# Routed attention and a cosine router on one Trainium2 core: weight sums in four 32-row strips, spread by GpSimd, and routing work in other turns

## The chip, the core and the metric

The kernel runs on one core of a Trainium2 chip. Its engines are TensorE (PE in the profile, with PEld for its weight loads), VectorE (DVE), ScalarE (ACT), GpSimd (POOL) and SyncE (SP, which here only issues DMAs). The metric is device time in microseconds (us), the median of the runs shown. Lower is better.

## What is computed

The input is four batches of eight heads, 768 tokens of width 64. Each query and each key is given to the nearest of 16 centroids of its head; a query attends only to keys of its own centroid. The result, as 3072 rows of width 512, goes to a router that picks one of eight experts by cosine similarity, and each row passes through the two layers of its expert.

```
mask   = q_assign[:, :, :, None] == k_assign[:, :, None, :]
scores = where(mask, scale * q @ k^T, -1e9)
attn   = exp(scores - max);  attn = attn / (sum(attn, axis=-1) + 1e-9)
x      = (attn @ v) as (B*S, H*D)
logits = x_n @ emb_n^T / tau;  e = argmax(logits);  gate = softmax(logits)[e]
out    = gate * (relu(x @ w1[e]) @ w2[e])
```

The part that the change touches is the denominator, the sum of the attention weights of each query, and the order in which the router's small operations are put between the attention's.

## The kernel before

**Tiling.** Two heads are taken together, which gives 16 pairs, numbered here 0 to 15; four pairs make a batch, and `n`, `nb` and `b` in the code are the pair, the pair within its batch and the batch. A pair's queries are cut into two halves of 384 columns. For each half there are six units, one for each block of 128 keys. Six units that belong to one half of one pair are a group; there are 32 groups, 0 to 31, and group 2n + half belongs to pair n. The main loop takes two units at a time. This text calls that a turn: a pair has turns 0 to 5 (`it` in the code), turns 0 to 2 for its first group and 3 to 5 for its second.

**A turn.** In a turn the code issues, in this order: the scores of the next two units (L355, key cluster match in bf16 and then the product in f32, both heads side by side) and their exponentials on ACT (L366); what `between` puts there; in some turns `divide`; then for the turn's own two units `attend` (L375, weights times v into `o_ps`, and DVE adds the weights into `acc`, L384 and L394); in turns 0 and 3 at the end, `total` of the group that has just ended. The order on PE, DVE and ACT is the order in which the code issues the work (a manual schedule); each engine works its queue in order. POOL's order is set by the scheduler.

**The denominator.** `total` (L397) multiplies `acc` by a matrix of ones with two matmuls, one for each head, whose 64 output rows all hold the same sums (L402). ACT copies the 128x384 result out of PSUM (L410) and DVE takes its reciprocal (L411) into `den`. `divide` (L419) multiplies `o_ps` by `den` into `xT`; `rows` (L436, L441) transposes `xT` into the rows `xr`. `o_ps` and the PSUM bank `misc` have two buffers each, `prob` has five, `acc` and `den` two. In the last pair, group 30's `divide` stands in turn 4 and its `rows` in turn 5; group 31's `total`, `divide` and `rows` come after the loop, between the first matmuls of the experts' layer (`hidden`, L739).

**What `between` places.** For the next pair: transposes of q and k (turns 5 and 0), sums of v on POOL and centroid products (turn 1), `assign` (turn 2: DVE L275 and L276, then a POOL product L277), `choose` (turn 3: DVE L283 and L284), one-hot transposes (turn 4). For the pair before: `rows` of its first group in turn 1, of its second in turn 2. For the batch before: `route_pieces`, that is `products` (L458), `norms` (ACT, L483), `logits` (L471, DVE L474), `choose` (five DVE operations L494 to L498, six POOL additions into `cumx` L500, a square root on ACT), `gate_scale` (four DVE operations L505 to L508), `gate_exp` and `gate_sum` (three DVE operations L515 to L517, and SP's DMA of the rows to `x_rows`, L518). In the last batch, pairs 14 and 15 also hold the first part of the sorting of tokens to experts (`early`): `ranks` (PE L548 and L555 read `cumx` and `eq`; DVE L563) in turn 3 of pair 14, `firsts` and `experts` (L573 to L606) in its turn 4, `dest` (L616 to L640) in its turn 5, `hot_blocks` and `hot_rows` (L650 to L658) in turns 0 to 2 of pair 15, and in its turn 3 `tokens` (L667, L676 to L680) and three indirect loads on POOL's queue (L695).

**After the loop** come 28 blocks of 128 tokens through `hidden` (L739, L746) and `result` (L755, L765, L766), with weights loaded by SP.

Of the kernel before, what the change touches and what calls it, by code (L numbers as in the profile page):

```python
# [9 lines left out]
F32 = mybir.dt.float32  # L10
# [8 lines left out]
P = 128  # L19
# [18 lines left out]
def kernel(  # L38
# [12 lines left out]
    nc = tc.nc  # L51

    B, H, S, D = q.shape
# [4 lines left out]
    NJ = S // P  # L58
    NHP = H // 2
    HS = S // 2  # L60
# [18 lines left out]
    const = ctx.enter_context(tc.tile_pool(name="const", bufs=1))  # L79
# [8 lines left out]
    embT = const.tile([P, KD, 2 * C], F32, name="embT")  # L88
    prefc = const.tile([P, C], BF16, name="prefc")
    prefe = const.tile([P, E], BF16, name="prefe")  # L90
    ones = const.tile([P, D], F32, name="ones")
    epsc = const.tile([P, 1], F32, name="epsc")
    io_i = const.tile([P, P], I32, name="io_i")
    io_b = const.tile([P, P], BF16, name="io_b")
# [20 lines left out]
    smp = ctx.enter_context(tc.tile_pool(name="smp", bufs=2))  # L115
# [14 lines left out]
    def misc():  # L130
        return psM.tile([P, 512], F32, tag="misc", name="misc")
# [4 lines left out]
    def load(n, names):  # L136
        b, hp = pairs[n]
        t = ld.setdefault(n, {})
        for nm in names:
            t[nm] = ldp.tile([P, NJ, 2, D], F32, tag=nm + "32", name=nm + "32")  # L140
            for h in range(2):
                nc.sync.dma_start(
                    out=t[nm][:, :, h],
                    in_={"q": q, "k": k, "v": v}[nm][b, 2 * hp + h].rearrange(
                        "(p j) d -> p j d", j=NJ
                    ),
                )
# [60 lines left out]
    bk = misc()  # L208
# [12 lines left out]
    bk = misc()  # L221
# [118 lines left out]
    GU = NJ  # L340
    units = [(n, hq, j) for n in range(len(pairs)) for hq in range(2) for j in range(NJ)]
    ngroups = len(units) // GU
# [54 lines left out]
    def total(g):  # L397

        d = gr[g]
        bk = misc()  # L400
        for h in range(2):
            nc.tensor.matmul(  # L402
                bk[D * h : D * h + D, 0:HS],
                lhsT=ones,
                rhs=d["acc"][:, h],
                start=True,
                stop=True,
            )
        d["den"] = smp.tile([P, HS], F32, tag="den", name="den")
        nc.scalar.copy(d["den"], bk[:, 0:HS])  # L410
        nc.vector.reciprocal(d["den"], d["den"])  # L411

    def divide(g):
        n, hq, _ = units[GU * g]
# [14 lines left out]
    def rows(g):  # L429

        n, hq, _ = units[GU * g]
        b, hp = pairs[n]
        U = NJ // 2
        bk = misc()
        for u in range(U):
            nc.tensor.transpose(  # L436
                bk[:, P * u : P * u + P], xT[b, hq][:, hp, P * u : P * u + P], ident
            )
        if b not in xr:
            xr[b] = xp.tile([P, NJ, XW], F32, tag="xr", name="xr")  # L440
        nc.scalar.copy(  # L441
            xr[b][:, U * hq : U * hq + U, P * hp : P * hp + P],
            bk[:, 0:HS].rearrange("p (u w) -> p u w", w=P),
        )
# [260 lines left out]
    def weights(j):  # L705
        part, c = (0, j) if j < KA else (1, j - KA)
        sp = (EngineType.SP,)
        e = nc.values_load(eblks[part][0:1, c : c + 1], engines=sp, min_val=0, max_val=E - 1)
        c = nc.values_load(echgs[part][0:1, c : c + 1], engines=sp, min_val=0, max_val=1)
        nc.sync.dma_start(  # L710
            out=w1s[j % 2],
            in_=moe_w1[ds(e, 1)].rearrange("o (c p) f -> p (o c) f", p=P),
            cond=c > 0,
        )
        nc.sync.dma_start(
            out=w2s[j % 2],
            in_=moe_w2[ds(e, 1)].rearrange("o (c p) d -> p (o c) d", p=P),
            cond=c > 0,
        )
# [60 lines left out]
    prepare, route = {}, {}  # L780
# [11 lines left out]
    def piece(n, name):  # L792
        if n < NP:
            if n not in prepare:
                prepare[n] = prep_pieces(n)
            prepare[n][name]()

    def between(n, it):
        b, nb = divmod(n, NHP)
        if it == 5:  # L800
            piece(n + 2, "turn0")
            if n + 1 == NP:
                route[b] = route_pieces(b)
                rows(2 * n)
                route[b][0](0)
        elif it == 0:
            piece(n + 1, "turn1" if n else "turn0")
        elif it == 1:
            piece(n + 1, "values")
            piece(n + 1, "products")  # L810
            if n > 0:
                rows(2 * n - 2)
        elif it == 2:
            piece(n + 1, "assign")
            if n > 0:
                rows(2 * n - 1)
        elif it == 3:
            piece(n + 1, "choose")
        elif it == 4:
            piece(n + 1, "hots")  # L820
        if b > 0:
            if nb == 0 and it == 3:
                route[b - 1] = route_pieces(b - 1)
                for half in range(2):
                    route[b - 1][0](half)
            j = NJ * nb + it - 3
            if 0 <= j < NJ:
                route[b - 1][2](j)
            if nb == 1 and it == 3:
                for half in range(2):  # L830
                    route[b - 1][1](half)
            if nb in (1, 2) and 0 <= j - NJ < 4:
                route[b - 1][3][j - NJ]()
        if b == B - 1 and (nb, it) in early:
            early[nb, it]()
        if b == B - 1 and (nb, it) == (3, 0):
            weights(0)
            weights(1)

    with tc.manual_schedule(engines={EngineType.PE, EngineType.DVE, EngineType.Activation}):  # L840
        for name in ("turn0", "turn1", "values", "products", "assign", "choose", "hots"):
            piece(0, name)
        load(1, "qk")
        for m in range(2):
            scores(m)
            expo(m)
        for i in range(0, len(units), 2):
            n, it = divmod(i // 2, NJ)
            if it == 0 and n + 1 < NP:
                load(n + 1, "v")  # L850
            if it == 4 and n + 2 < NP:
                load(n + 2, "qk")
            if it == 0 and n == 1:

                for w in range(2):
                    nc.sync.dma_start(
                        out=w1s[w], in_=moe_w1[0].rearrange("(c p) f -> p c f", p=P)
                    )
                    nc.sync.dma_start(
                        out=w2s[w], in_=moe_w2[0].rearrange("(c p) d -> p c d", p=P)  # L860
                    )
            for m in range(i + 2, min(i + 4, len(units))):
                scores(m)
                expo(m)
            between(n, it)
            if i % GU == 2 and i > GU:
                divide(i // GU - 1)
            if i + 2 == len(units):
                ats.close()
                tile_waits = {"side": "right", "reuse_waits": "tile"}  # L870
                psX = ctx.enter_context(tc.tile_pool(name="psX", bufs=1, space=PSUM, **tile_waits))
                turn_x(0, nc.scalar.copy, xp.tile([P, DM], F32, tag="acc", name="xTm"))
            for m in range(i, i + 2):
                attend(m)
            if i % GU == 0 and i > 0:
                total(i // GU - 1)
            if i == 0:
                piece(1, "turn1")
        at.close()
        mop = ctx.enter_context(tc.tile_pool(name="mop", bufs=2, **tile_waits))  # L880
        rtb = ctx.enter_context(tc.tile_pool(name="rtb", bufs=1, **tile_waits))
        psH = ctx.enter_context(tc.tile_pool(name="psH", bufs=3, space=PSUM, **tile_waits))

        products, logits, norms, (choose, *gates) = route[B - 1]
        pb = Places(1, rtb)
        hidden(0, (0,))
        total(ngroups - 1)
        divide(ngroups - 1)
        for j in range(NJ // 2):
            norms(j)  # L890
        hidden(0, (1,))
        turn_x(1, nc.scalar.copy)
        logits(0)
        rows(ngroups - 1)
        products(1)
        hidden(1, (0,))
        for j in range(NJ // 2, NJ):
            norms(j)
        logits(1)
        choose()  # L900
        hidden(1, (1,))
        for gate in gates:
            gate()
        fetch(3)
        turn_x(2, nc.scalar.copy)
        result(0, (0,))
        pb.ranks()
        pb.firsts()
        result(0, (1,))
        weights(2)  # L910
        pb.dest()
        pb.experts()
        hidden(2)
        pb.hot_blocks()
        pb.hot_rows(0, 1)
        result(1, (0,))
        turn_x(3, nc.scalar.copy)
        result(1, (1,))
        weights(3)
        hidden(3, (0,))  # L920
        pb.tokens()
        hidden(3, (1,))
# [72 lines left out]
```

## Time and profile before

| what | us |
|---|---|
| median of 3 runs | 855.54 |
| the runs | 854.64, 855.54, 858.0 |
| the profiled execution, its own time | 857.06 |
| its span in the profile | 855.3 |
| attention loop, from the first scores to the last group | about 20 to 434 |
| the experts' layer | about 430 to 855 |

| engine | busy us | share of the span |
|---|---|---|
| PE | 828.1 | 97% |
| PEld | 491.2 | 57% |
| DVE | 362.5 | 42% |
| ACT | 305.5 | 36% |
| POOL | 126.5 | 15% |

All times of the profile are of that one execution, in us from the start of its span unless marked ns. A matmul of f32 operands shows as two records, since PE makes two passes; the counts of the PE groups are of passes. A group of the profile is one line, engine and shape; its mean is that of one record. In a timeline the bracket behind a row is the time that the engine sat idle before it and what ended that. The granted clock of PE (PEclk) is a share of its full speed.

### The profile page before, as it was taken

What the parts mean: (1) busy time and instruction counts of PE and PEld (TensorE: products, weight loads), DVE (VectorE), ACT (ScalarE), POOL (GpSimd) and SP (SyncE); (2) the same over time, 40 slices, a digit from 0 to 9 for tenths busy, and PEclk for the clock granted to TensorE, in tenths of its full rate; (3) what the DMA queues carried; (4) which work ended last, traced back from release to release, by engine and by line L of the source; (5) the groups of instructions that cost most, each with busy time, mean ns of one, the idle gap of its engine ahead of it and who ended that gap; (6) DMA issues with size and microseconds to landing.
All of it is one profiled execution on the core that took longest, in us unless ns stands there. A gap on an engine that the chain in (4) does not pass through costs nothing.

```text
span 855.3 us, 12807 instructions
## 1 busy us (share of the span) xinstructions
PE 828.1 (97%) x5227; PEld 491.2 (57%) x5227; DVE 362.5 (42%) x521; ACT 305.5 (36%) x489; POOL 126.5 (15%) x172
## 2 busy tenths in 40 slices
PE   4999999999999999999899999999999999999995
PEld 2444444444444444444386767767676767767672
DVE  3577878787868877789835000000000000000000
ACT  3555556755567555665452111111111111111110
POOL 4010111211112111020101101011110101010100
PEclk9999999999999999999999999999999999999998
DMA  9922211242211422011127847748383747216410
GB/s 238 342 56 57 56 31 25 57 130 57 56 34 23 130 56 57 20 47 47 33 105 295 291 177 260 290 144 319 125 321 141 289 173 273 95 47 250 184 38 22
DMA packets 108781, 115.24 MB, mean 135 GB/s; under 512 B 77221, under 2 KB 77221, under 8 KB 108208
## 3 DMA queue, kind: packets, MB, share of 16 engines
q1 hardware_dynamic: 104064, 100.68, 37.0%
q0 software_dynamic: 4480, 13.65, 4.2%
q8 instruction: 43, 0.70, 0.3%
q14 instruction: 18, 0.15, 0.1%
q10 hardware_dynamic: 176, 0.05, 0.0%
HBM read 152.11 MB, written 13.64 MB: 194 GB/s over the span
## 4 chain that ended last, share of the span: by engine, by line
PE 49%; issue 25%; DMA 22%; DVE 2%; SPq 0%; POOL 0%; ACT 0%; POOLq 0%
PE s_ps L355 19%; DMA out_dram<-y,sidx 17%; PE o_ps L375 16%; PE misc L239 3%; DMA out_dram<-y,gidx 3%; PE misc L402 2%; PE h_ps L739 2%; DMA w1s<-in_moe_w_dram 2%; PE misc L436 2%; PE misc L297 1%; PE misc L254 1%; PE misc L267 1%; PE y_ps L755 1%; PE misc L458 1%; DVE den L411 1%
## 5 line engine op out<-in xcount | busy, mean ns | idle before, releaser
L739 PEld LDWEIGHTS h_ps<-xTm,w1s 128*128 128x128 f32 x1792 | 202.5, 192 | 24.2 <-DVE xTm L727 20.5
L739 PE MATMUL h_ps<-xTm,w1s 128*128 128x128 f32 x1792 | 207.9, 277 | 2.8 <-DMA w1s<-in_moe_w_dram 2.8
L755 PE MATMUL y_ps<-w2s,hT 128*128 128x512 f32 x448 | 201.1, 592 | 0.0
L366 ACT ACTIVATE prob<-s_ps 128x768 f32<-128x768 f32 x192 | 153.9, 810 | 125.2 <-PE s_ps L355 97.6
L727 DVE COPY xTm<-x_ps 128x512 f32<-128x512 f32 x24 | 16.6, 691 | 333.4 <-PE x_ps L725 333.4
L355 PE MATMUL s_ps<-qT,kT 64*128 64x384 f32 x768 | 157.7, 489 | 0.0
L375 PE MATMUL o_ps<-prob,v 128*64 128x384 f32 x768 | 145.1, 499 | 0.0
L394 DVE TENSOR_TENSOR acc<-acc,prob 128x768 f32<-128x768 f32 x128 | 129.8, 1014 | 3.6
L755 PEld LDWEIGHTS y_ps<-w2s,hT 128*128 128x128 f32 x448 | 81.0, 190 | 81.8 <-issue 81.8
L746 ACT ACTIVATE hT<-h_ps 128x512 f32<-128x512 f32 x56 | 33.4, 597 | 201.3 <-PE h_ps L739 201.3
L411 DVE RECIPROCAL den<-den 128x384 f32<-128x384 f32 x32 | 81.7, 2552 | 31.2 <-ACT den L410 31.2
L355 PEld LDWEIGHTS s_ps<-qT,kT 64*128 64x128 f32 x768 | 69.6, 191 | 22.1 <-issue 22.1
L375 PEld LDWEIGHTS o_ps<-prob,v 128*64 128x64 f32 x768 | 46.6, 136 | 54.0 <-issue 53.1
L765 ACT ACTIVATE y<-y_ps,xin 128x512 f32<-128x512 f32 x28 | 19.2, 687 | 150.3 <-PE y_ps L755 139.1
L766 POOL DMA_INDIRECT out_dram<-y,sidx x24 | 24.0, 1001 | 292.5 <-ACT y L765 286.6
L355 PE MATMUL s_ps<-qH,kH 64*128 64x384 bf16 x384 | 64.1, 331 | 1.0 <-ACT kH L306 0.9
L355 PEld LDWEIGHTS <-kH 64*128 64x128 bf16 x384 | 19.0, 94 | 70.8 <-issue 48.2
L313 POOL TENSOR_TENSOR vs<-v 128x384 f32<-128x384 f32 x16 | 16.4, 1025 | 202.5 <-DMA v<-in_v_dram 202.5
L277 POOL TENSOR_TENSOR sel<-sel,prefc 128x384 bf16<-128x384 bf16 x16 | 24.2, 1514 | 110.2 <-DVE sel L276 110.2
L695 POOL DMA_INDIRECT xin<-x_rows,gidx x28 | 29.7, 1059 | 33.4 <-DVE gidx L680 12.4
L248 DVE COPY kT<-misc 128x384 f32<-128x384 f32 x32 | 17.8, 556 | 36.0 <-PE misc L239 36.0
L384 DVE SCALAR_TENSOR_TENSOR acc<-prob 128x768 f32<-128x768 f32 x32 | 30.3, 946 | 0.0
(183 smaller groups left out, 499.3 us busy)
## 6 DMA issues: line engine op xcount, KB each, us to landing
w1s<-in_moe_w_dram SPq DMA_DIRECT2D x30, 2048.0 KB
w2s<-in_moe_w_dram SPq DMA_DIRECT2D x30, 2048.0 KB
x_rows<-xr SPq DMA_DIRECT2D x4, 1539.0 KB
q<-in_q_dram SPq DMA_DIRECT2D x32, 192.0 KB
k<-in_k_dram SPq DMA_DIRECT2D x32, 192.0 KB
v<-in_v_dram SPq DMA_DIRECT2D x32, 192.0 KB
xin<-x_rows,gidx POOLq DMA_INDIRECT x28, 7.2
out_dram<-y,sidx POOLq DMA_INDIRECT x24, 6.8
```

The lines of the kernel that those rows point to most:

```text
L239: nc.tensor.transpose(bk[:, P * j : P * j + P], t[nm][:, NJ // 2 * half + j].rearrange("p h d -> p (h d)"), ident,)
L277: nc.gpsimd.tensor_tensor(sel, sel, bc(prefc, shp, 1), ALU.mult)
L355: nc.tensor.matmul(s_ps[:, h, 0:HS], lhsT=t[l][rows, P * j : P * j + P], rhs=t[r][rows, HS * hq : HS * hq + HS], start=first, stop=not first,)
L366: nc.scalar.activation(d["prob"], d["s_ps"][:, :, 0:HS], ACTF.Exp)
L375: nc.tensor.matmul(g["o_ps"][D * h : D * h + D, 0:HS], lhsT=ld[n]["v"][:, j, h], rhs=d["prob"][:, h], start=(j == 0), stop=(j == NJ - 1),)
L384: nc.vector.scalar_tensor_tensor(out=g["acc"], in0=un[i - 1]["prob"], scalar=NJ * EPS, in1=d["prob"], op0=ALU.add, op1=ALU.add,)
L394: nc.vector.tensor_tensor(g["acc"], g["acc"], d["prob"], ALU.add)
L411: nc.vector.reciprocal(d["den"], d["den"])
L695: nc.gpsimd.indirect_dma_start(out=xin, out_offset=None, in_=x_rows[0:n], in_offset=bass.IndirectOffsetOnAxis(ap=gidxs[part][:, c : c + 1] ...
L739: nc.tensor.matmul(bk[:, m : m + P], lhsT=w1s[j % 2][:, c, f0 + m : f0 + m + P], rhs=d["xT"][:, P * c : P * c + P], start=(c == 0), stop=( ...
L746: nc.scalar.activation(d["hT"][:, f0 : f0 + 512], bk, ACTF.Relu)
L755: nc.tensor.matmul(bk, lhsT=d["hT"][:, P * c : P * c + P], rhs=w2s[j % 2][:, c], start=(c == 0), stop=(c == KF - 1),)
```

## The change

`total` computes four matmuls of 192 columns and 32 output rows in place of two of 384 columns and 64 rows: strip i holds the sums of one head's half of the columns, 32 equal rows. The ACT copy and the reciprocal then run on 128x192 elements. `den` still has to be 128x384, so eight POOL copies of 32x192 each write every strip to its own 32 rows and to the other 32 rows of its head. `divide` moves one turn later (turns 2 and 5 in place of 1 and 4), but for group 30; for group 31 it stays right behind its `total`. `rows` of a pair's second group moves from turn 2 to turn 3 of the next pair. The route pieces of the batch before move from (pair within the batch, turn): `products` of both halves at (0, 3) to one at (0, 3) and one at (1, 2); both `logits` at (1, 3) to (1, 3) and (2, 2); `norms` start one turn later; `choose`, `gate_scale`, `gate_exp`, `gate_sum` from (1, 3), (1, 4), (1, 5), (2, 0) to (2, 2), (2, 3), (2, 4), (2, 5).

```diff
@@ tile constants
-    ones = const.tile([P, D], F32, name="ones")
+    ones = const.tile([P, D // 2], F32, name="ones")
@@ def total(g):
+        W = HS // 2
         bk = misc()
-        for h in range(2):
+        for i in range(4):
             nc.tensor.matmul(
-                bk[D * h : D * h + D, 0:HS],
+                bk[D // 2 * i : D // 2 * i + D // 2, 0:W],
                 lhsT=ones,
-                rhs=d["acc"][:, h],
+                rhs=d["acc"][:, i // 2, W * (i % 2) : W * (i % 2) + W],
                 start=True,
                 stop=True,
             )
+        inv = smp.tile([P, W], F32, tag="inv", name="inv", bufs=1)
+        nc.scalar.copy(inv, bk[:, 0:W])
+        nc.vector.reciprocal(inv, inv)
+
         d["den"] = smp.tile([P, HS], F32, tag="den", name="den")
-        nc.scalar.copy(d["den"], bk[:, 0:HS])
-        nc.vector.reciprocal(d["den"], d["den"])
+        for i in range(4):
+            for to in (i, i ^ 1):
+                nc.gpsimd.tensor_copy(
+                    d["den"][D // 2 * to : D // 2 * to + D // 2, W * (i % 2) : W * (i % 2) + W],
+                    inv[D // 2 * i : D // 2 * i + D // 2],
+                )
@@ def between(n, it):
         elif it == 2:
             piece(n + 1, "assign")
+        elif it == 3:
+            piece(n + 1, "choose")
             if n > 0:
                 rows(2 * n - 1)
-        elif it == 3:
-            piece(n + 1, "choose")
...
             if nb == 0 and it == 3:
                 route[b - 1] = route_pieces(b - 1)
-                for half in range(2):
-                    route[b - 1][0](half)
-            j = NJ * nb + it - 3
+            products, logits, norms, choices = route.get(b - 1, (None,) * 4)
+            j = NJ * nb + it - 4
             if 0 <= j < NJ:
-                route[b - 1][2](j)
-            if nb == 1 and it == 3:
-                for half in range(2):
-                    route[b - 1][1](half)
-            if nb in (1, 2) and 0 <= j - NJ < 4:
-                route[b - 1][3][j - NJ]()
+                norms(j)
+            if (nb, it) == (0, 3):
+                products(0)
+            elif (nb, it) == (1, 2):
+                products(1)
+            elif (nb, it) == (1, 3):
+                logits(0)
+            elif (nb, it) == (2, 2):
+                logits(1)
+            if nb == 2 and it >= 2:
+                choices[it - 2]()
@@ main loop
-            if i % GU == 2 and i > GU:
+            if i > GU and i % GU == (4 if i // GU + 1 < ngroups else 2):
                 divide(i // GU - 1)
```

## The prediction

> **What bounds the kernel now.** First the table by stage, for what is full in the steady attention loop (100 to 160 us) and at its end (400 to 420).
>
> ```profile
> core 0: us, PE busy (x) PEld busy (x) DVE busy (x) ACT busy (x) POOL busy (x), PEclk, DMA share, GB/s
> 100.00:160.00 60.00, 60.00 (x421) 27.85 (x419) 45.64 (x50) 35.75 (x61) 8.81 (x11) 1.00 0.28 60
> 400.00:420.00 20.00, 17.83 (x104) 7.53 (x102) 18.64 (x39) 8.20 (x12) 0.36 (x1) 0.91 0.00 1
> ```
>
> PE is full in the loop. From the starts of the scores in the timeline (200.26, 204.87, 209.29, 213.26, 217.06, 221.17, 225.14) turns 0 to 5 last 4.61, 4.42, 3.97, 3.80, 4.11 and 3.97 us, and every pair without routing repeats this to 0.01: only what PE itself does counts there. From 400 to 420 DVE is full, PE has gaps and the granted clock falls to 0.91. So a total is worth its PE time in most pairs; in pairs 14 and 15 DVE's queue decides. Next the timeline around one total (204) and around products on 32 output rows (206).
>
> ```profile
> 203.47 0.81 PE L375 MATMUL o_ps<-prob,v 128*64 128x384 f32 x4
> 204.12 0.81 PE L402 MATMUL misc<-acc,ones 128*64 128x384 f32 x4
> 204.87 0.34 PE L355 MATMUL s_ps<-qH,kH 64*128 64x384 bf16 x2
> 205.85 0.81 PE L355 MATMUL s_ps<-qT,kT 64*128 64x384 f32 x4
> 206.59 0.52 PE L254 MATMUL misc<-qT,cnB 128*32 128x384 f32 x2
> 206.93 0.49 PE L254 MATMUL misc<-qT,cnB 128*32 128x384 f32 x2
> 207.37 0.33 PE L436 MATMUL misc<-ident,xT 128*128 128x128 f32 x1
> ```
>
> A pass of 384 columns streams 0.32 us, two strips at once: a total takes two, 0.65 us. Four strips of 32 rows also run side by side (L254: passes at 206.59 and 206.93, 0.345 apart). Where the strip shape changes, a gap is added: the last scores pass starts at 206.17 (205.85 + 0.32) and L254 at 206.59, 0.42 later, so 0.10 is lost; L402 (204.44) to L355 (204.87) and L254 (206.93) to L436 (207.37) lose 0.10 too; L375 to L402, of one shape, none. Then rows for durations (source views: ns min/median/max), and the chain of waits late in the last pair.
>
> ```profile
> L411 DVE RECIPROCAL den<-den 128x384 f32<-128x384 f32 x32 | 81.7, 2552 | 31.2 <-ACT den L410 31.2
> L315 POOL TENSOR_TENSOR vs<-vs x16: 452/454/458, 10.3 to 385.1; 128x128 f32<-128x128 f32 x16
> masks.py:199 POOL TENSOR_SCALAR_AFFINE_SELECT ident<-ident x1: 282/282/282, 1.1 to 1.1; 128x128 f32<-128x128 f32 x1
> L277 POOL TENSOR_TENSOR sel<-sel,prefc x16: 907/1554/1559, 15.9 to 391.6; 128x384 bf16<-128x384 bf16 x16
> L394 DVE TENSOR_TENSOR acc<-acc,prob x128: 937/957/1483, 29.8 to 429.7; 128x768 f32<-128x768 f32 x128
> ```
> ```profile
> 422.24 0.67 PE misc L402 x4
> 422.93 0.49 ACT den L410
> 423.44 2.55 DVE den L411
> 426.03 0.63 DVE xT L419
> 426.70 0.55 PE misc L436 x3
> ```
>
> Here the denominator is itself the path: PE waits for group 30's `xT`.
>
> **PE's gain.** A new total streams two passes of 192 columns, 0.32 in all, plus 0.02 of skew (0.345 against 0.32), plus one more change of shape after L375, 0.10. So 0.65 becomes 0.44: 0.20 saved. Bounds: 0.15 if a short pass doesn't cover the next weight loads (four of 0.11), 0.30 if going from 64 to 32 rows costs nothing. Totals 0 to 27 lie where PE decides: 28 x 0.20 = -5.6 us (-4.2 to -8.4). [...] `rows`, `products` and `logits` keep their PE time and only move.
>
> **A POOL copy, 32x192 f32, isn't in the trace.** One input, 128 elements: 282 ns (the select). POOL's fills give a slope of 0.8 ns per element (1368 for 1536, 151 for 12), so at least 0.30 with 0.15 fixed; two f32 inputs give 2.1 (454 for 128, 995 for 384), so at most 0.59. I take 0.34, by the select row plus 64 elements. Fills issue 0.05 before the one ahead ends, so eight take 8 x 0.29 = 2.35 us (1.95 to 4.3). ACT's copy falls from 0.48 to 0.33 (0.79 ns per element from its 384 and 512 rows), the reciprocal from 2.55 to 1.36 (0.19 at 6 elements, 6.24 ns each).
>
> **Why this stays hidden in most pairs.** PE ends total at 204.6, ACT at 205.1, DVE at 206.5. The copies then meet two `acc` additions. The L277 and L394 rows show these taking turns: POOL's product is 907 alone and 1554 beside an addition, the second addition 1483 beside it. So eight copies may last from 206.5 to 211 (2.35 + two additions). The moved `divide` stands behind L276, at 212.7: 1.7 us in hand. Behind it on DVE are two additions, ending near 215.6 with POOL's L277 in between; turn 3's total reads this `acc` and its records start at 216.32, so with the added change of shape it is needed at 216.4. Turn 4's copies run from 219.2 to 224.1, `divide` is due at 224.4. On POOL the sums of v are ahead of turn 1's copies and L277 is behind them, ready at 212.8 as before. The moved `rows` takes ACT to 216.4, still before total's copy at 217. Nothing is lost. If copies cost over 0.6 each this cover is gone. [...]
>
> **Pair (b, 2), turn 2.** Now `logits` and `choose` (0.26 + 1.14 on DVE, from L474 and the starts 444.78 to 445.92) stand ahead of `divide` and the additions, and six `cumx` additions on POOL (0.28 apart; 848 instead of 198 behind an addition) push between them. `acc` is ready 5.1 after amax, needed at 4.8 (216.4 less 211.59): +0.3 in pairs 6 and 10, +0.6.
>
> **Pair 14 is worse.** The chain of waits of before goes PE total 28 (395.51), ACT, reciprocal (396.71 to 399.26), then DVE alone until total 29 at 408.75, where PE sat idle 2.17 us. New on DVE: 0.26 + 1.14 in turn 2, `gate_scale` 0.8 (448.14 to 448.87) in turn 3, `gate_sum` 0.65 (450.25 to 450.88) in turn 5; off it 1.2 of reciprocal. Laid out from amax at 390.38: additions end 395.6, one-hots 396.65, gate_scale 397.45, ranks 398.1, group start 399.05, reciprocal 400.4 (was 399.26), turn 4's additions 404.75 (404.03), gate_sum 405.35, dest 408.1, divide and additions 410.6 (408.70). So total 29 starts 1.9 later. Also PE's `ranks` now reads a `cumx` made one turn earlier: its last three additions wait behind the second `acc`, so it is ready near 396.3, with PE there at 394.2. That 2.1 is mostly swallowed by the wait at total 29, but the one-hots' transposes come late and hold DVE 0.45. Sum +2.35 (0.5 to 4.5), less 0.2 for total 29. The `x_rows` DMA goes onto SP's queue at 405 instead of 383, ahead of the expert weights issued from 403.38, which move nothing (DMA share 0.00 from 400 to 420); the first gather that reads `x_rows` is at 421.7, so this costs nothing as long as 1.5 MB land in some 15 us.
>
> **Group 30 in pair 15 is the largest loss.** `divide` isn't moved, and POOL's order puts the three gathers of turn 3 ahead of the eight copies; in the trace of before these end at 425.96. Copies: 426.0 to 428.4, divide 0.62, rows at 429.1 instead of 426.70: +2.4 (1.7 to 4.4). Behind the waiting `divide` DVE has four `acc` additions (4.06 us), done at 433.1 and needed by total 31 near 436: no second loss. PE is idle 3.1 us. After the 2.17 us at 408 the matmuls lasted up to 0.84 instead of 0.48 and one scores-rows-attend stretch took 5.28 (409.55 to 414.83) against 3.64 for the next: 1.64 lost at a low granted clock. I add +1.64 (0 if it isn't triggered).
>
> **Group 31.** From the first L402 at 433.76: PE 0.40, ACT 0.33 (start at +0.6), reciprocal to +2.3, copies to +4.75, divide to +5.4, rows at +5.47; before, rows stood at 438.88, +5.12. So +0.35 (-0.3 to +2.3).
>
> **Sum.** -5.6 + 0.6 + 2.35 - 0.2 + 2.4 + 1.64 + 0.35 = +1.5 us. The profiled execution (857.06; 1.8 outside its span of 855.3) would become 858.6. It is 1.5 above the median of 855.54, so the same step on the median gives **857.0**. The experts' layer only shifts.
>
> **The rivals.**
> *Faster:* strips change shape for nothing, cumx slips through and the clock holds: -8.4 + 0 + 1.65 - 0.3 + 1.7 + 0 - 0.3 = -5.6, so 850. For it: every turn of PE's is full, so each tenth per total is 3 us. Against: all three changes of shape that I measured cost 0.10.
> *Slower:* the copies cost the two-input rate. Each 0.1 per copy adds 0.8 at group 30 and 0.8 at group 31, so at 0.59 it is +4, 861. It decides above 0.6: then turn 3's total waits for `acc` in each pair, 0.8 us for each further 0.1, times 15; at 0.8 that is another 24, 885. For it: no copy on POOL, nor one that shifts rows, is in the trace. Against: the fill and select rows lie low.
> *The change doesn't do what it says:* four strips run one after another, 8 x 0.16 = 1.3 us per total, +0.75 x 31 = +23, 879. L254 speaks against it.
>
> **How the numbers follow.** Forecast 0.50, faster 0.14, slower 0.33, strips in a row 0.03. About 0.5% (4.3 us) is what a measurement of this kernel can tell from no change. All low ends together give 849 (-8.4 + 0.3 + 0.5 - 0.2 + 1.7 + 0 - 0.3 = -6.4), all high ends 865 (-4.2 + 1 + 4.5 - 0.2 + 4.4 + 1.64 + 2.3 = +9.4, the second term bounded by 0.3 and 1); few fall together, so 851 to 862 is the forecast's own range. For the copies near the two-input rate the range reaches to 866, which leaves some 0.1 on either side. Faster by over 0.5%: 0.14; within: 0.51; slower: 0.35.
>
> **What would show it.** Turns 0 and 3 shorter by 0.2 apart from the moved rows; copies of 0.34 us, taking turns with L394; `divide` without a wait in pairs 1 to 13; PE's wait at total 29 ending about 1.9 later against the total before it; group 30's rows 7 us after its total, with a low granted clock behind. It is wrong if copies exceed 0.6 us, if a total saves under 0.1 or over 0.3, or if pairs 1 to 13 show waits that repeat.

## The result and the profile after

| | before | after |
|---|---|---|
| median, us | 856.28 (6 runs, 854.64 to 858.0) | 866.61 (6 runs, 865.51 to 868.4) |
| ratio of the medians | | 1.0121 [1.0101, 1.0140] |
| profiled execution, its own time / span, us | 857.06 / 855.3 | 865.62 / 863.8 |
| PE busy, us (share) | 828.1 (97%) | 825.2 (96%) |
| DVE busy | 362.5 (42%) | 326.2 (38%) |
| ACT busy | 305.5 (36%) | 299.7 (35%) |
| POOL busy | 126.5 (15%) | 245.2 (28%) |

The changed kernel is 1.2% slower, where 857.0 was forecast with a range up to 866. PE has 3 us less to do and DVE 36 us less, yet the span is 8.5 us longer. The table by stage of the changed kernel shows where.

```profile
core 0: us, PE busy (x) PEld busy (x) DVE busy (x) ACT busy (x) POOL busy (x), PEclk, DMA share, GB/s
100.00:160.00 60.00, 60.00 (x443) 27.16 (x443) 40.54 (x51) 34.98 (x60) 27.09 (x51) 1.00 0.26 58
400.00:420.00 20.00, 16.31 (x124) 7.23 (x124) 17.43 (x40) 8.19 (x12) 6.00 (x11) 1.00 0.20 80
420.00:430.00 10.00, 4.90 (x36) 1.75 (x32) 3.35 (x6) 2.88 (x5) 4.93 (x8) 0.85 0.30 79
430.00:440.00 10.00, 8.05 (x44) 4.54 (x45) 4.36 (x5) 1.55 (x3) 1.03 (x3) 0.64 0.00 0
```

In the steady loop PE is still full, and POOL has 27 us of work in 60 where it had 9. Between 420 and 440 PE is empty for seven of the twenty microseconds and its granted clock falls to 0.64; before, the same two windows had PE at 9.34 and 9.98 of 10 with a clock of 1.00. Most of the loss is there.

**The steady loop.** From the starts of the scores, turns 0 to 5 of a pair without routing last 4.43, 4.42, 3.64, 4.10, 4.11 and 3.97 us, 24.67 together; before it was 4.61, 4.42, 3.97, 3.81, 4.11 and 3.97, 24.89. The timeline of one such pair (engine by engine; PE unless marked) shows the new pieces.

```profile
205.44 4.25 POOL L417 COPY den<-inv 32x192 f32<-32x192 f32 x8 [6.92 <-DVE inv L412]
...
211.28 0.61 DVE L428 SCALAR_TENSOR_TENSOR xT<-o_ps,ev,den 128x384 f32<-128x384 f32 x1
...
213.27 0.55 PE L445 MATMUL misc<-ident,xT 128*128 128x128 f32 x3
213.74 1.51 PE L375 MATMUL o_ps<-prob,v 128*64 128x384 f32 x8
215.18 0.53 PE L403 MATMUL misc<-acc,ones 128*32 128x192 f32 x8
215.65 0.34 PE L355 MATMUL s_ps<-qH,kH 64*128 64x384 bf16 x2
```

The eight copies end at 209.69, `divide` (L428) comes 1.6 us later without a wait. The total (L403) takes 0.47 from its start to the next scores, where it took 0.75 before; 0.10 of this goes to the new change of shape behind `attend` (1.44 from the start of `attend` to the total, 1.34 before), and the turn is 0.18 shorter. But `rows` (L445) now stands alone between scores and `attend`: turn 2, which lost it, fell by 0.33, and turn 3, which got it, rose by 0.48 (4.10 against 3.62 in pair 0, which has no `rows` there). The rows of the source views for the new operations (ns min/median/max) and, from the view of the copies, who waited for them (us, times):

```profile
L412 DVE RECIPROCAL inv<-inv x32: 1339/1353/1355, 40.9 to 442.4; 128x192 f32<-128x192 f32 x32
...
L417 POOL COPY den<-inv x256: 332/342/1072, 42.4 to 446.5; 32x192 f32<-32x192 f32 x128
...
  DVE xT L428: 12.5, 3
```

Only three of the 32 `divide` ever waited for a copy: those of groups 29, 30 and 31.

**Pairs 14 and 15.** The timeline:

```profile
390.37 2.99 POOL L509 TENSOR_TENSOR cumx<-cumx,eq 128x8 bf16<-128x8 bf16 x6 [0.84 <-DVE eq L507]
...
393.41 0.23 PE L557 MATMUL misc<-cumx,onesb 128*128 128x152 bf16 x1 [1.92 <-POOL cumx L509]
...
407.22 1.51 PE L375 MATMUL o_ps<-prob,v 128*64 128x384 f32 x8 [2.62 <-DVE xT L428]
409.07 0.53 PE L403 MATMUL misc<-acc,ones 128*32 128x192 f32 x8 [0.35 <-DVE acc L394]
...
412.63 5.52 POOL L417 COPY den<-inv 32x192 f32<-32x192 f32 x8 [3.01 <-DVE inv L412]
```

Pair 14 starts 2.9 us earlier than before (376.16 against 379.04), loses 1.92 to PE's wait for `cumx`, and then waits for DVE as it did before, only in another place: at group 30's first `attend`, whose `o_ps` buffer the late `divide` of group 28 has to free. At the scores of pair 15's turn 4 the changed kernel is still 1.1 us ahead (421.68 against 422.81).

Part of that lead comes from the clock. In the kernel before, the granted clock was at half behind the wait of 2.17 us at group 29's total, and turn 1 of pair 15 lasted 5.28 us there; in the changed kernel it is 3.64 at full clock, 1.64 less. The row of the kernel before:

```profile
core 0: us, PE busy (x) PEld busy (x) DVE busy (x) ACT busy (x) POOL busy (x), PEclk, DMA share, GB/s
409.90:413.20 3.30, 3.30 (x13) 1.37 (x11) 3.30 (x3) 1.51 (x3) 0.00 (x0) 0.50 0.00 0
```

**Group 30.** The timeline of the changed kernel from its total to the experts' first matmuls:

```profile
421.21 0.53 PE L403 MATMUL misc<-acc,ones 128*32 128x192 f32 x8
...
422.11 1.26 POOL L704 DMA_INDIRECT xin<-x_rows,gidx  x1 [3.96 <-issue]
...
423.67 1.00 POOL L704 DMA_INDIRECT xin<-x_rows,gidx  x1 [0.31 <-issue]
...
424.97 0.99 POOL L704 DMA_INDIRECT xin<-x_rows,gidx  x1 [0.30 <-issue]
426.01 0.71 POOL L417 COPY den<-inv 32x192 f32<-32x192 f32 x2
...
428.90 2.25 POOL L417 COPY den<-inv 32x192 f32<-32x192 f32 x6 [2.17 <-DMA xin<-x_rows,gidx]
...
431.19 0.62 DVE L428 SCALAR_TENSOR_TENSOR xT<-o_ps,ev,den 128x384 f32<-128x384 f32 x1 [7.62 <-POOL den L417]
...
431.95 0.87 PE L445 MATMUL misc<-ident,xT 128*128 128x128 f32 x3 [7.05 <-DVE xT L428]
...
437.66 3.84 PE L748 MATMUL h_ps<-xTm,w1s 128*128 128x128 f32 x32
```

The same steps in the kernel before:

```profile
422.07 0.81 PE L402 MATMUL misc<-acc,ones 128*64 128x384 f32 x4
...
426.70 0.55 PE L436 MATMUL misc<-ident,xT 128*128 128x128 f32 x3 [0.66 <-DVE xT L419]
...
429.99 3.84 PE L739 MATMUL h_ps<-xTm,w1s 128*128 128x128 f32 x32
```

From total to `rows` it was 4.63 us before and is 10.74 now. The three gathers stand ahead of the copies in POOL's queue, and after two copies POOL stops for 2.17 us until the gathers' data have landed. The source view of the copies shows what it stops at, a semaphore instruction at 428.8 (POOLq is POOL's sequencer):

```profile
L417 POOLq EVENT_SEMAPHORE  x1: 43/43/43, 428.8 to 428.8; - x1
```

In the trace this instruction and the third copy behind it wait for the three semaphores that the gathers raise when they land; the copies go on at 428.90. So the wait is an instruction of the built program, not something that POOL's queue does by itself. PE waits 7.05 us. Behind that, 5.71 us pass from `rows` to the first `hidden` matmuls, against 3.29 before; the granted clock is 0.50 from 427.0 to 437.2. So 1.1 us ahead becomes 7.7 us behind (first `hidden` 437.66 against 429.99). Group 31 adds 0.9 (the second block's `hidden` 448.88 against 440.29), and the experts' layer only shifts.

### The profile page after: what moved, and what is told of

Same layout as the page of the kernel before. It is cut to its first block, busy times and chain, and to the rows that moved or that the text cites. A ratio compares the mean times of both kernels' runs of the same rounds, so it can differ in the third digit from the quotient of the medians.

```text
span 863.8 us, 13383 instructions
## 1 busy us (share of the span) xinstructions
PE 825.2 (96%) x5355; PEld 487.3 (56%) x5355; DVE 326.2 (38%) x521; ACT 299.7 (35%) x489; POOL 245.2 (28%) x428
## 4 chain that ended last, share of the span: by engine, by line
issue 25%; DMA 22%; PE 3%; POOL 1%; DVE 0%; POOLq 0%; ACT 0%; SPq 0%
DMA out_dram<-y,sidx 17%; DMA out_dram<-y,gidx 3%; DMA w1s<-in_moe_w_dram 2%; PE h_ps L748 1%; PE y_ps L764 1%; POOL den L417 1%; DMA xin<-x_rows,gidx 0%; PE o_ps L375 0%; PE misc L467 0%; PE x_ps L734 0%; PE misc L445 0%; DVE inv L412 0%; POOL xin L704 0%; DVE xT L428 0%; POOLq L704 0%
## 5 line engine op out<-in xcount | busy, mean ns | idle before, releaser
L417 POOL COPY den<-inv 32x192 f32<-32x192 f32 x256 | 123.5, 482 | 117.0 <-DVE inv L412 105.1
L412 DVE RECIPROCAL inv<-inv 128x192 f32<-128x192 f32 x32 | 43.3, 1352 | 25.0 <-ACT inv L411 24.7
```

Of the source, the lines that this page charges most:

```text
L412: nc.vector.reciprocal(inv, inv)
L417: nc.gpsimd.tensor_copy(d["den"][D // 2 * to : D // 2 * to + D // 2, W * (i % 2) : W * (i % 2) + W], inv[D // 2 * i : D // 2 * i + D // 2],)
```

## The experiments

In all of them the kernel before ran on the same chip, at medians of 856.0 to 856.8. A "wide" total in the list is four strips of 32 rows over all 384 columns: both pairs of strips then hold a whole head's sums, so the result lies where `den` needs it, and no POOL copies follow; ACT's copy and the reciprocal have their old size.

| kernel | median us | ratio, 95% interval |
|---|---|---|
| changed kernel | 866.61 | 1.0121 [1.0101, 1.0140] |
| group 30 wide | 858.53 | 1.0015 [1.0005, 1.0026] |
| gathers behind group 30's copies | 864.55 | 1.0099 [1.0083, 1.0114] |
| before, all totals wide | 861.0 | 1.0054 [1.0038, 1.0071] |
| before, rows moved alone | 862.17 | 1.0066 [1.0044, 1.0088] |
| total of before, all turns moved | 863.86 | 1.0081 [1.0062, 1.0100] |
| changed, routing in old turns | 868.27 | 1.0127 [1.0109, 1.0145] |
| narrow strips, all in old turns | 864.33 | 1.0099 [1.0084, 1.0114] |
| changed, rows in turn 4 | 871.96 | 1.0182 [1.0169, 1.0196] |
| the same, 30 and 31 wide, divide 28 early | 863.58 | 1.0085 [1.0072, 1.0099] |
| the same, routing in old turns | 859.85 | 1.0047 [1.0033, 1.0060] |
| narrow strips, rows half a pair later | 852.61 | 0.9952 [0.9938, 0.9965] |

**1. Group 30 without copies.**

```diff
 def total(g):
+        if g == ngroups - 2:   # four strips, rhs=acc[:, i // 2], 0:HS; copy and reciprocal into den
+            ...
+            return
```

> Only group 30 differs from the changed kernel: its sums are taken over all 384 columns in four strips, ACT copies 128x384 and DVE takes the reciprocal of it, so no POOL copy stands between its total and its divide. Theory (most of the loss is group 30: copies behind three gathers and their landing, then a slow clock): rows of group 30 come 4.7 us after its total instead of 10.7, the stretch from these rows to the first hidden matmul takes 3.3 instead of 5.7, so the time is about 8 us under the changed kernel: 858 to 859, ratio to before 1.002. Rival (the strips and copies cost something all along, or what is won there is lost again in the experts' layer): 863 or more.

858.53: as expected. One group out of 32 accounts for 8.1 of the 10.3 us. The timeline (in this kernel L403 is the wide total, L459 `rows`, L762 `hidden`):

```profile
423.34 0.85 PE L403 MATMUL misc<-acc,ones 128*32 128x384 f32 x8
...
428.12 0.52 PE L459 MATMUL misc<-ident,xT 128*128 128x128 f32 x3 [0.77 <-DVE xT L442]
...
431.38 3.84 PE L762 MATMUL h_ps<-xTm,w1s 128*128 128x128 f32 x32
```

Total to `rows` is 4.78, and `rows` to `hidden` 3.26, as in the kernel before (4.63 and 3.29): with the long idle stretch the low clock behind it goes too (1.00 from 420 to 440; `hidden`'s first block takes 3.84 in both).

**2. The gathers behind group 30's copies.** POOL's queue in the order of the code, and the three gathers issued after the copies.

```diff
-        (3, 3): lambda: (pa.tokens(), fetch(0), fetch(1), fetch(2)),
+        (3, 3): lambda: pa.tokens(),
...
-    with tc.manual_schedule(engines={EngineType.PE, EngineType.DVE, EngineType.Activation}):
+    with tc.manual_schedule(engines={EngineType.PE, EngineType.DVE, EngineType.Activation, EngineType.Pool}):
...
                 total(i // GU - 1)
+            if i == GU * (ngroups - 1):
+                for j in range(3):
+                    fetch(j)
```

> The changed kernel, with POOL's queue in the order of the code and the first three gathers issued after group 30's total, so that its eight copies stand ahead of them on POOL. Theory (group 30's copies are late because the three gathers and a wait for their landing stand ahead of them): rows of group 30 come some 6.1 us after its total instead of 10.7, the first gather then lands about 9 us after the total and the first transpose of expert input waits for it, so half of the loss remains: 861 to 862, ratio 1.006. Rival (the copies are late for their own cost or for DVE): rows stay 9 us or more behind the total, 865 or more.

864.55, partly as expected: the wait inside the copies went, and the one it left behind cost more than was allowed for. The timeline:

```profile
423.90 3.02 POOL L417 COPY den<-inv 32x192 f32<-32x192 f32 x8 [5.48 <-DVE inv L412]
...
427.73 0.52 PE L445 MATMUL misc<-ident,xT 128*128 128x128 f32 x3 [2.55 <-DVE xT L428]
...
431.03 1.09 PE L734 MATMUL x_ps<-ident,xin 128*128 128x128 f32 x4 [2.00 <-DMA xin<-x_rows,gidx]
...
434.81 4.90 PE L748 MATMUL h_ps<-xTm,w1s 128*128 128x128 f32 x32
```

The eight copies run without a break in 3.02, and `rows` come 6.25 after the total (421.48) instead of 10.74. But the gathers are now late themselves, PE waits 2.00 for `xin`, and the granted clock falls again (0.50 from 430.3 to 437.0; behind the wait `attend` takes 2.83 instead of 1.51 and `hidden`'s first block 4.90 instead of 3.84). Copies and gathers both want POOL at that moment; either order costs several microseconds (864.55 and 866.61 against 858.53 without the copies).

**3. What a change of tile shape costs.** The kernel before with every total wide: the same number of columns per strip, two strips more, nothing else.

```diff
-        for h in range(2):
+        for i in range(4):
...
-                bk[D * h : D * h + D, 0:HS],
+                bk[D // 2 * i : D // 2 * i + D // 2, 0:HS],
...
-                rhs=d["acc"][:, h],
+                rhs=d["acc"][:, i // 2],
```

> The kernel before with every total as four strips of 32 rows over all 384 columns: the same streaming time on PE as two strips of 64 rows, ACT and DVE as before, no POOL copies. Theory (a change of strip shape between attend and total costs about 0.12 us): turns 0 and 3 rise from 4.61 and 3.81 to 4.73 and 3.93, 31 times, +3.7 us: 860, ratio 1.0043. Rival (the change of shape is free, and the strips of 192 columns saved 0.18 instead of 0.32 for another reason): turns unchanged, 856.6.

861.0. Turns 0 and 3 last 4.75 and 3.94 against 4.61 and 3.81: going from 64-row to 32-row strips costs 0.13 to 0.14 per total. The prediction's 0.12 (0.10 and 0.02 of skew) was nearly right.

**4. `rows` moved alone.** The kernel before with the second group's `rows` in turn 3.

```diff
             piece(n + 1, "assign")
-            if n > 0:
-                rows(2 * n - 1)
         elif it == 3:
             piece(n + 1, "choose")
+            if n > 0:
+                rows(2 * n - 1)
```

> The kernel before with one edit: rows of the second group go from turn 2, next to the transposes of assign, to turn 3, where they stand between scores and attend. Theory (transposes that stand alone pay one more change of tile shape on PE): turn 2 falls from 3.97 to 3.64 us and turn 3 rises from 3.81 to 4.29, so 0.15 us in each of 15 pairs, +2.2 us: 858.5, ratio 1.0026. Rival (moving them is free, and a strip total saves only 0.04): turn 3 becomes 4.14, time 856.3.

862.17, 3.7 above the expectation. The steady part is as expected: turn 2 is 3.64 (was 3.97) and turn 3 is 4.28 (was 3.81), +0.14 per pair. That the price hangs on the neighbours shows in turn 1 too: in the kernel before it lasts 4.42 with `rows` behind the 32-row products and 3.94 in pair 0, which has no `rows` there, again 0.48. The excess is in the pairs with routing: turn 3 of (b,1) lasts 6.11 against 4.61. The timeline there:

```profile
268.83 0.55 PE L436 MATMUL misc<-ident,xT 128*128 128x128 f32 x3
269.22 0.49 PE L471 MATMUL misc<-ident,pT 128*128 128x128 f32 x3
...
270.66 0.55 PE L471 MATMUL misc<-ident,pT 128*128 128x128 f32 x3 [0.95 <-DVE lg L474]
```

`rows` and the two `logits` are three users of the two `misc` buffers in one turn, and the third waits 0.95 until one is read out. So the routing had to move with `rows`.

**5. All the moves, with the total of before.**

```diff
 def total(g):
+        ...   # two matmuls, ACT copy and reciprocal into den, as in the kernel before
+        return
```

> All moved turns of the change with the total of before (two matmuls of 64 rows, ACT copy and reciprocal over 384 columns, no POOL copies). Theory: no PE time saved by strips (0.19 in 28 totals), rows alone +2.2, pair 14 delayed by 2.8 us of routing work on DVE with the full reciprocal; group 30 as before: +5 to +6 us, 861 to 862, ratio 1.006. Rival (the strips or copies alone make the loss): 857.

863.86, 2 to 3 above the expectation: the moves alone, without strips or copies, make the kernel 0.8% slower. A plain pair lasts 25.04 instead of 24.89, turn 3 of pair 14 lasts 6.67 instead of 4.04 (the wait for `cumx`), and turns 3 and 4 of (b,2) are 0.36 and 0.43 longer than in a plain pair. Against 856.65 for the kernel before on that chip the moves cost 7.2 us. The prediction's terms for them, 0.6 and 2.35, make 2.95, though the 2.35 counts on a reciprocal 1.2 us shorter, which this run doesn't have.

**6. The routing in its old turns.** The changed kernel with `products`, `logits`, `norms` and choices where they were before.

> The changed kernel with the route pieces in their old turns (products, logits, norms, choose and the gates as before); strips, copies, late divide and rows in turn 3 stay. Theory (the moved choose and gates delay pair 14): turn 3 of pair 14 falls from 6.55 to about 4.3 us, because cumx is ready long before ranks, and DVE has 2.8 us less to do before group 28's divide, so group 30's first attend starts about 2.8 us earlier. Group 30's long wait stays. Time about 863.5, ratio 1.009. Rival (pair 14's delay is hidden by what follows, or the old turns cost as much in batches 1 to 3): 866 or more.

868.27, a miss; the rival held (866 or more, the old turns costing as much in batches 1 to 3). Turn 3 of pair 14 fell from 6.55 to 4.55 as expected, but turn 3 of (b,1) rose from 4.43 to 6.42, three times: the collision of run 4.

**7. `rows` back in turn 2, `divide` at the head of that turn.** Narrow strips with copies for groups 0 to 29, 30 and 31 wide, routing as before.

```diff
+            if i > GU and i % GU == 4 and i // GU + 1 < ngroups:
+                divide(i // GU - 1)
             between(n, it)
-            if i > GU and i % GU == (4 if i // GU + 1 < ngroups else 2):
+            if i // GU + 1 == ngroups and i % GU == 2:
                 divide(i // GU - 1)
```

> A version made from the findings: strips of 192 columns and POOL copies for groups 0 to 29; groups 30 and 31 without copies (four strips over 384 columns); divide of the late groups at the head of turns 2 and 5, ahead of assign and of the sorting work; rows of second groups back in turn 2 next to assign; route pieces in their old turns. Theory (strips gain 0.18 per total, everything else lost was the order around them): turns 0 and 3 of each pair 0.18 shorter than before, turn 2 as before, pair 14 at most 24.3, so 30 x 0.18 = 5.4 and about 1 us of DVE time in pair 14: 850, ratio 0.992 to 0.994. Rival (late denominators make new waits wherever they are put): 856 or more.

864.33, a miss; the rival held. Turns 0 and 3 are 4.43 and 3.62, but turn 2 of pairs 1 to 14 lasts 4.48 to 5.42 in place of 3.97. The timeline of one that lasts 4.97:

```profile
210.48 3.74 POOL L431 COPY den<-inv 32x192 f32<-32x192 f32 x8
...
214.26 0.62 DVE L442 SCALAR_TENSOR_TENSOR xT<-o_ps,ev,den 128x384 f32<-128x384 f32 x1 [2.91 <-POOL den L431]
...
215.02 0.52 PE L459 MATMUL misc<-ident,xT 128*128 128x128 f32 x3 [0.81 <-DVE xT L442]
```

The copies end at 214.2, too late for a `rows` in this turn, and DVE waits with them. So with these copies on POOL `rows` can't keep turn 2 of the next pair without a wait.

**8. `rows` in turn 4, beside other 128x128 tiles.** The changed kernel, then also with 30 and 31 wide and group 28's `divide` ahead of `dest`, then also with the routing in its old turns (second `products` at (0, 5)).

```diff
         elif it == 3:
             piece(n + 1, "choose")
-            if n > 0:
-                rows(2 * n - 1)
         elif it == 4:
             piece(n + 1, "hots")
+            if n > 0:
+                rows(2 * n - 1)
```

> The changed kernel with rows of a pair's second group in turn 4, behind the one-hots' transposes, in place of turn 3. Theory (rows dear in turn 3 because nothing else there uses 128x128 tiles, so they bring one more change of tile shape): turn 3 falls from 4.10 to 3.62 and turn 4 rises from 4.11 to 4.44 only, a plain pair lasts 24.52 instead of 24.67, pair 14 starts near 373.9 instead of 376.16, and in pair 15 the tokens no longer wait 0.7 for group 29's divide: 863.5. Rival (0.15 is the price of rows standing ahead of attend, wherever): turn 4 is 4.59, a plain pair stays at 24.67, and the time is 866.

> As the one with rows in turn 4, and besides groups 30 and 31 with wide totals (four strips over 384 columns, no GpSimd copies) and the divide of group 28 ahead of dest in turn 5 of pair 14. Theory: 858.5 as measured with group 30 alone wide, less 2.2 for rows, less 1.1 for group 31, less 1 to 2 for the wait of 2.6 at group 30's first attend: 853.5 to 854.5. Rival (what PE wins up to pair 14 only makes it wait longer for VectorE in pairs 14 and 15, since that queue decides there): 856.5 or more, with group 30's total as far behind the start of pair 14 as before.

> As the one before, but with the routing in its old turns (both logits at (1, 3), choose and gates from there; only the second products at (0, 5), since its rows come in turn 4). Theory: (b,1) turn 3 holds no rows, so nothing collides there; choose no longer stands in pair 14, so its turn 3 falls from 6.5 to about 4.5 and DVE has 3.2 us less in pair 14: 851.5 to 853. Rival: the two logits in one turn cost what the ones apart save, and pair 15 takes the rest: no faster than the kernel with the routing in its new turns.

871.96, 863.58 and 859.85: all three miss their theories. The first is beyond its rival too, the second lies where its rival put it (856.5 or more), and the third is faster than the second, against its rival. Turn 3 fell to 3.62, as expected, but turn 4 rose to 4.80, where 4.44 (theory) or 4.59 (rival) was expected. The timeline of turn 4 in the first of them (the middle row is PE's, the last its weight load):

```profile
219.63 0.84 PE L297 MATMUL misc<-identb,oh 128*128 128x128 bf16 x12
...
220.31 0.34 PE L320 MATMUL misc<-epsc,vs 128*128 128x1 f32 x2
...
220.79 0.31 PEld L445 LDWEIGHTS misc<-ident,xT 128*128 128x128 f32 x3 [0.23 <-DVE qH L303]
```

The one-hots and the sums of v take both `misc` buffers, so `rows` are a third user and wait until DVE has read the one-hots. Both theories had priced tile shapes and overlooked the buffers. The third kernel has the same at (0, 5), where the `products` are a third user: that turn lasts 5.36 instead of 3.97. What the second and third do show: with the routing in its old turns, pair 14 falls from 27.32 to 24.61.

**9. `rows` half a pair later.** Turn 1 and turn 2 are the two places where, before, `rows` stood beside one other piece without a wait. Here they hold `rows` that are older: the second group's go to turn 1 of the pair after next, the first group's to turn 2 of the next. `xT` has three buffers, each with one half of the queries of a whole batch, so it can wait. 30 and 31 are wide, the routing is in its old turns (norms one turn later), `divide` of group 28 is ahead of `dest`, `rows(29)` in turn 4 of pair 15.

```diff
         elif it == 1:
...
-            if n > 0:
-                rows(2 * n - 2)
+            if n > 1:
+                rows(2 * n - 3)
         elif it == 2:
             piece(n + 1, "assign")
+            if n > 0:
+                rows(2 * n - 2)
         elif it == 3:
             piece(n + 1, "choose")
-            if n > 0:
-                rows(2 * n - 1)
```

> Narrow strips and copies for groups 0 to 29, wide totals for 30 and 31, divide as in the changed kernel (but ahead of dest for group 28), and the transposes of rows where they stood beside other work before, only a pair later: second groups' in turn 1 of the pair after next, first groups' in turn 2; the routing in its old turns, norms one turn later. So rows never stand alone in a turn nor where both buffers of misc are taken, and every xT is half a pair old when they come. Theory: a plain pair lasts 4.43 + 4.42 + 3.97 + 3.62 + 4.11 + 3.97 = 24.52 against 24.89 before, (b,0) and (b,1) 0.37 less than before too, no wait on divide; pair 14 starts near 373.9 against 379.04, and its turn 3 has no wait for cumx. Group 30 as before: 850 to 852. Rival (the narrow total cannot be had without a loss elsewhere): waits for misc or DVE show in turns 1 to 4, or pairs 14 and 15 give back what is won, 855 or more.

852.61, ratio 0.9952 [0.9938, 0.9965]: faster than both kernels, 0.6 above the range expected. A plain pair lasts 24.52, turn by turn as written; (b,0) 25.95 and (b,1) 25.35 against 26.32 and 25.74 before. The timeline of PE around turn 2, and further down the start of the experts:

```profile
208.61 0.55 PE L267 MATMUL misc<-ident,asT 128*128 128x128 f32 x3
208.99 0.49 PE L459 MATMUL misc<-ident,xT 128*128 128x128 f32 x3
209.41 1.51 PE L375 MATMUL o_ps<-prob,v 128*64 128x384 f32 x8
...
425.26 3.84 PE L762 MATMUL h_ps<-xTm,w1s 128*128 128x128 f32 x32
```

Pair 14 starts at 374.19, 4.85 ahead of before; its turn 3 is 3.86 with no wait for `cumx`; and `hidden` starts 4.73 ahead, so the lead is kept to the end. Several things are changed together against the changed kernel, so this run shows that the narrow total can pay, not what each of them is worth.

## Why the prediction was wrong, point by point

**Where the time was lost: right.** Group 30 was named the largest loss, by the gathers ahead of the copies in POOL's queue. Run 1 shows it.

**The copy's price and the saving per total: right.** 0.342 us at the median for 0.34 forecast; the reciprocal 1.353 for 1.36, ACT's copy 0.318 for 0.33. A total saves 0.18 for 0.20 (4.61 to 4.43 in turn 0). No `divide` waited in pairs 1 to 13. So the rival of copies at the two-input rate, the rival of strips that run one after another, and the faster one all fall; the result of 866.6 lies beyond the first of these (861), by another mechanism. Only the spacing of the copies was off, which counts at groups 30 and 31.

**The step that failed most: group 30, "+2.4" and "+1.64".** The place and the order in POOL's queue were right; the size was not, and one wait was missing. `rows` were put at 7.03 after the total and came at 10.74, so the delay was 6.11 in place of 2.4. The 3.7 between them: 0.86 since the gathers end later after the total (most of it, 0.67, since the index that they read, `gidx`, is ready later: its steps stand on DVE behind the `divide` of group 29, which waited 1.77 for copies that took 5.52 us beside DVE's additions); 2.17 for the wait in the middle of the copies until the gathers have landed, which the prediction didn't have at all; 0.65 since copies start 0.38 apart (eight in 3.01) and not 0.29. Run 2 shows the wait gone when the gathers stand behind. The low clock then cost 2.4 (5.71 less 3.29) in place of 1.64. Together 8.5 where 4.04 stood: 4.5 of the 7.0 us by which the profiled execution (865.62) missed its 858.6. Of the rest, some 2 come before pair 14 (`rows`, below) and 0.6 from group 31.

On the clock: in the 7.05 us without a matmul the granted clock fell to 0.50 at 427.0, 2.1 us after PE had gone idle, and stayed there until 437.2:

```profile
core 0: us, PE busy (x) PEld busy (x) DVE busy (x) ACT busy (x) POOL busy (x), PEclk, DMA share, GB/s
424.90:427.00 2.10, 0.00 (x1) 0.00 (x0) 0.00 (x0) 0.00 (x0) 1.66 (x3) 1.00 0.71 192
427.00:437.20 10.20, 5.25 (x21) 2.19 (x23) 4.36 (x5) 1.55 (x3) 2.04 (x6) 0.50 0.07 21
```

Behind three shorter waits the matmuls were slow too, and about 1.6 us were lost each time: 2.17 in the kernel before (5.28 for turn 1 of pair 15 against 3.64, at 0.50), 2.82 in run 9 (5.23 against 3.64 for the same stretch) and 1.93 in run 1 (4.30 from `attend` to the second scores against 2.72). In the changed kernel 2.62 and 0.35 close together left the clock at 1.00 (from 400 to 420), and so did the very wait of 2.17 us at group 29's total in run 3:

```profile
core 0: us, PE busy (x) PEld busy (x) DVE busy (x) ACT busy (x) POOL busy (x), PEclk, DMA share, GB/s
413.90:417.30 3.40, 3.40 (x27) 1.52 (x29) 3.37 (x5) 2.09 (x4) 0.36 (x1) 1.00 0.00 0
```

So in these runs a shorter wait sometimes cost clock and sometimes not, and the length of the wait alone doesn't tell which: the 1.64 that the prediction took from the wait at 408 was a price for that one wait, not a rule.

**"`rows`, `products` and `logits` keep their PE time and only move": wrong.** Moved out of a turn where L267 already uses 128x128 tiles, `rows` cost 0.48 in place of 0.33. That takes back 0.15 of the 0.36 that two totals save per pair; with the routing's moves pair 14 started 2.9 ahead, where 4.8 was forecast (27 totals of 0.20, less 0.6). The prediction had measured this very price, 0.10 for a change of shape, and applied it to the totals but not to the moved piece. Run 4 shows it alone, and in run 9 it is gone: there turn 3 holds no `rows` (3.62), and those in turn 2 stand beside L267 again (3.97).

**Pairs 14 and 15: the sum came out near, in part by luck.** PE's wait for `cumx` was put at 2.1 and is 1.92. But it was not "mostly swallowed" by the wait at total 29: that one shrank to 0.35 and PE's wait moved to group 30's first `attend` (2.62), which was not forecast. Up to the end of pair 15's turn 0 the two pairs lost 2.9 us where 1.95 was forecast (+2.35, less 0.2 for total 29 and 0.2 for total 27). That they had lost only 1.7 at turn 4 is luck: the 1.64 that the kernel before loses at half clock in turn 1 was spared, and no term of the sum has that. The sign that the prediction named for this, total 29 some 1.9 later against the total before it, failed: it is 0.6, since the wait for `cumx` holds back total 28 as well.

**Group 31: +0.35 was forecast, `rows` come 1.0 later after their total** (6.22 against 5.23; the 5.12 of the prediction takes the last transpose of `logits` at 438.88 for the first of `rows` at 438.99). The excess of 0.65 is the copies' spacing: the eight take 3.01 (443.84) where 2.35 was forecast.

**What stays open.** Why the built program makes POOL wait for the gathers at that place; the copies read and write nothing of `xin`, and the code of the kernel doesn't ask for it. It isn't bound to group 30: in runs 1 and 2 the first POOL copies behind the gathers are group 31's, and the same semaphore instruction stands ahead of them (437.6 and 442.0), where the gathers have long landed and it costs nothing. In the kernel before no POOL operation follows the gathers that closely. Open too is when a short wait brings the clock down to 0.50.

## What to carry to other kernels

Price a moved piece by its neighbours in the new place: the same three transposes cost 0.33 us beside tiles of their own shape, 0.48 where nothing else in the turn has their shape, and 0.69 as the third user of two buffers. Where a loop's last round is exposed, give it the form with the shortest chain, even if the others use the one with the least work: one group in 32 held 8 of the 10 us. And before work is put on an engine that is idle on average, look at what its queue holds at the one moment when the result is waited for.

## What the runs showed of the hardware that was not expected

- POOL copies of 32x192 f32 take 0.34 us alone and up to 1.07 beside DVE's `acc` additions; eight take 3.01 alone, 4.25 in a steady turn and 5.52 in pair 15. They start 0.38 apart, where POOL's fills had started 0.05 before the end of the one ahead.
- A change of tile shape on PE was seen at 0.10 (L254 before), 0.13 to 0.14 (run 3) and 0.15 us (run 4).
- PE's granted clock was 0.50 for 3.4 us (409.84 to 413.25) behind a wait of 2.17 us in the kernel before, and stayed at 1.00 behind an equal wait at the same total in another kernel (run 3).
